# Layer 1's last 1024 tokens as one group of two halves, with seven products in place of eight

## The chip, the cores and the metric

The kernel runs on one core of a Trainium2 chip, as one program. The core has a matrix engine (TensorE, PE in the profile; its weight loads are PEld), three engines for vectors (VectorE = DVE, ScalarE = ACT, GpSimd = POOL), and SyncE (SP), which in this kernel issues every DMA transfer on one queue, in its program's order. The metric is device time in microseconds, the median of several runs.

## The reference

Sliding-window attention over 4 x 8 heads, 576 positions, head dimension 64, then two layers on the 2304 tokens (model size 512, inner size 2048):

```python
rel = pos[:, None] - pos[None, :]
mask = (rel >= 0) & (rel < 64)
attn = softmax(where(mask, scale * q @ k.T, -1e9))
x = (attn @ v).transpose(0, 2, 1, 3).reshape(2304, 512)
h = np.maximum(x @ w_in, 0.0);  x = h * h @ w_out          # layer 1
h = x @ w_in2;  out = (h * np.cos(h)) @ w_out2             # layer 2
```

All of it is float32. The kernel reaches that on TensorE with values split in two (hi, rounded to the engine's format fp32r, and lo, the difference): each product of two matrices is three passes, hi x hi, hi x lo and lo x hi. "Three passes" below means this.

## The kernel before

**Order of the work.** A class `Plan` holds every step with its engines, an estimated length, a key and its dependencies, and takes, engine by engine, the step that can begin first (near ties: by key). The result is a fixed order of instructions for each engine; at run time an engine waits at an instruction until its inputs are there, and everything behind waits with it. Buffers come from rings (`Ring`). The ring "W" has 18 slots of 8 KB per partition and holds all weights, raw words of weights and large working tiles; "g" and "r" (activations) have two buffers each, "x2" two; PSUM has four "acc" and four "q" banks. DMA completions use eight semaphores in turn.

**Units of layer 1.** The tokens go in units of 256: attention for unit n runs in two passes g (`attention`: S on L639, exponentials on L662, transposes T on L681, weighted sums O on L696), and its result X, hi and lo, feeds the first product. Layer 1 works on spans of units: (0, 2 units), (2, 1), (3, 2), (5, 2), (7, 2), that is 512, 256, 512, 512, 512 tokens. For each of 16 blocks j of 128 inner elements, `g1` makes ph (L1208: 4 blocks of model size x three passes = 12 matmuls of up to 512 columns), `UnitA.act` makes g, hi and lo (L778 to L791), and two items later `g2` adds the block to four accumulators accA (L814: 4 x 3 = 12 matmuls). At the end of a span `finish` copies accA to x2 tiles (L834, L836) and stores them to DRAM (x2_dram, in the profile x_dram, L839). Weight block j is loaded as raw 64-bit words (L336), turned to float32 (`to_f32`: two passes on ScalarE at L347 and L307, a shift and a merging custom instruction on VectorE, L359 and L363) and split (`convert_w`: hi by a cast, L307 or L311, lo at L385). A weight tile of layer 1 holds the in and out weights of one j, 16 tiles in all, kept for the whole layer.

**Layer 2** works on three pairs of 768 tokens (two halves of 384). There the first product of two blocks j goes by seven products in place of eight (Strassen's scheme in Winograd's form): the weights of the two blocks, cut in 2 x 2, are turned into seven combined pieces, four in w2a and three in w2b, and the tokens into seven pieces B11, B21, T2, T1, T3, T4, B22 (`prepare`). `convert_w2` makes w2a, w2b and the out weights w2o of two blocks during the last spans of layer 1 and stores them in DRAM (L433, L503, L509); layer 2 loads them step by step as wa, wb and wo (`load_w`, L955). `group` (L1099) runs the products x, y, z of one step in three PSUM banks: ScalarE copies x to "held" (L1115), VectorE adds it to y or z (L1122), and x goes on accumulating. Activations of the first half are used at once, those of the second half are kept in SBUF and used behind the group. `Job` (L1057) is the second product into accB.

**The lines that matter for PE** are L1208 with L814 (spans of layer 1), L1099 and L1057 (layer 2). The list of spans and the place of the attention units in it:

```python
spans = [(0, 2), (2, 1)] + [(n, 2) for n in range(3, NUA, 2)]
att_at = {0: [1], N2 - 4: [2], N2: [3, 4]}
for s in range(2, NSA - 1):
    n, k = spans[s + 1]
    att_at[N2 + (s - 1) * NJ] = list(range(n, n + k))
```

Of the kernel before, what the change touches and what calls it, by code (L numbers as in the profile page):

```python
# [28 lines left out]
def f32(ap):  # L29
    return ap.bitcast(F32)  # L30
# [56 lines left out]
class Plan:  # L87
# [12 lines left out]
    def op(self, engs, key, fn, deps=(), take=(), use=(), lat=None, gap=0, order=()):  # L100
# [96 lines left out]

START = {'ahead': 3,
# [31 lines left out]
def kernel(  # L230
# [10 lines left out]
    w2o: bass.AP,  # L241
    seq: int,
# [14 lines left out]
    TW = 2 * H  # L257
    NPAIR = NT // TW
# [22 lines left out]
        "pb": Ring(1), "sm": Ring(2), "PT": Ring(1), "br": Ring(2), "bg": Ring(2), "R": Ring(4), "h": Ring(2),  # L281
    }
# [91 lines left out]
    def convert_w(src, j, key, late, after, early):  # L374
# [15 lines left out]
        w_hi[j] = [hi, hi]  # L390
        w_lo[j] = [lo, lo]
        w_buf[j] = wb

    w2_half = {}
# [3 lines left out]
    def convert_w2(j, key, after):  # L398

        jp, q = divmod(j, 2)  # L400
        w2_half[q] = to_f32(w2, j, key, [after, w2_taken[0]], key - 3, True, False)
        if not q:
            return
        (wa, ba, oa), (wb_, bb, ob) = w2_half[0], w2_half[1]
        cvs, t = [ba, bb], {}
        bufs = {x: R["W"].buf() for x in "oab"}
# [10 lines left out]
        def oh(e, i):  # L417
            if i == 0:
                new("o", [2, 2, DM])
            copy(e, t["o"][:, i, 0], (wa, wb_)[i]()[:, 1])  # L420

        def ol(e, i):
            sub(t["o"][:, i, 1], (wa, wb_)[i]()[:, 1], f32(t["o"][:, i, 0]))

        ends = []
        prev = None
        for i in range(2):
            h = op(both(DM), key, lambda e, i=i: oh(e, i), [(oa, ob)[i], prev],
                   [] if i else [bufs["o"]], [*cvs, *([bufs["o"]] if i else [])])
# [59 lines left out]
        def blo2(e):  # L489
# [4 lines left out]
        o1 = op(d, key, s1, [oa, ob, *ends], A, cvs)  # L494
# [8 lines left out]
        st.append(dma(key, lambda e: nc.sync.dma_start(w2a[jp], f32(t["a"])), P * 8 * Q * 4,  # L503
                      [l1, l2], use=A))
# [9 lines left out]


# [33 lines left out]
    def mask_kind(t):  # L549
# [11 lines left out]
    spans = [(0, 2), (2, 1)] + [(n, 2) for n in range(3, NUA, 2)]  # L561
    x_col = [0, UA, 2 * UA] + [((n - 3) % 4) * UA for n in range(3, NUA)]
    x_before = [
        [m for m in range(n) if x_col[m] == x_col[n]][-1:] for n in range(NUA)]
# [4 lines left out]
    def attention(n, g, key, sp, k_s=None):  # L569
# [156 lines left out]

        half, off = divmod(x_col[n], 2 * UA)
        sl = slice(off, off + UA)
        cs = slice(2 * g, 2 * g + 2)
# [21 lines left out]
    class UnitA:  # L751
# [56 lines left out]
        def g2(self, j, m, t, w):  # L808
# [40 lines left out]
    class Half:  # L849
# [20 lines left out]
        def g2(self, j, m, t, w):  # L870
# [25 lines left out]
    def piece_free(p, o, c):  # L896
# [3 lines left out]
        for i in (4 * o + 2 * c, 4 * o + 2 * c + 1):  # L900
            out.append(open_b[0] if 10 <= i < 18 else g1_last[NUA - 3 if i < 10 else NUA - 1])
        return out

    def prepare(p, at, key, after):
        t0 = p * TW
        for c in range(2):
# [38 lines left out]
            split(B22, 3, l)  # L945

# [217 lines left out]

    def job_at(p, k):
        return base + p * 22.7 + 16.8 + 0.376 * (2 + k)

    units = [UnitA(n, k) for n, k in spans]
    NSA = len(spans)
# [14 lines left out]
    base = place[-1] - LAG + 1.0  # L1184
    N2 = NJ + J0
    att_at = {0: [1], N2 - 4: [2], N2: [3, 4]}
    for s in range(2, NSA - 1):
        n, k = spans[s + 1]
        att_at[N2 + (s - 1) * NJ] = list(range(n, n + k))

    w2_at, done = {}, 0
    for i in range(NA):
        if done >= 26 and len(w2_at) < NJ and done >= 26 + 6 * len(w2_at):
            w2_at[i] = len(w2_at)
        done += items[i][0].w // UA
    line = [None]

    def g1(i, key):
        u, j = items[i]
        phb, wb = R["q"].buf(), w_buf[j]  # L1200
        t = {}
        for c in range(NCC):
            def mm(e, c=c):
# [3 lines left out]
                for k, (wl, xl) in enumerate(((0, 0), (0, 1), (1, 0))):  # L1207
                    nc.tensor.matmul(  # L1208
                        t["ph"][:, 0:u.w], wb.tile[:, 0, wl, c * P:c * P + P], u.x(xl, c),
# [4 lines left out]
                         [line[0], w_hi[j][0], w_lo[j][0], *u.x_ready(c)],  # L1214
# [7 lines left out]
    def g2(i, key, g, ends=None, part=None):  # L1222
        u, j = items[i]
        t, gb, ready = g
        wb = w_buf[j]
        ends = [] if ends is None else ends
        for m in range(u.groups) if part is None else part:
            def mm(e, m=m):
# [4 lines left out]
                         [line[0], w_hi[j][1], w_lo[j][1], *ready], take, [gb, wb, *use],  # L1233
# [9 lines left out]
    for j in range(NJ):  # L1243
        key = 2.0 * (j if j < SK else 2 * j - SK) - 6.0
        key, late, early = START["conv"].get(j, (key, key, key - 3.0))
        convert_w(w1, j, key, late, w_lo[j - 4][1] if j >= 4 else None, early)
    gs = {}

    def att_key(n, g):
        if (n, g) in START["att"]:  # L1250
            return START["att"][n, g]
        if n <= 4:
            return 16.0 + 8.0 * (n - 2) + 4.0 * g, 2.0
# [186 lines left out]
```

## Time and profile before

| | us |
|---|---|
| median of three runs | 854.56 |
| the three runs | 854.49 to 854.81 |
| span of the profiled execution | 852.8 |
| PE busy in it | 845.4 |
| VectorE busy | 589.8 |
| ScalarE busy | 489.2 |
| end of layer 1's last span on PE, about | 469 |

The profile is of one execution; its span is the time between the first and the last instruction that it records, and it has no other time of its own. The granted clock is that of TensorE. The rows on which the argument rests stand in a section of their own below.

### The profile page before, as it was taken

What the parts mean: (1) busy time and instruction counts of PE and PEld (TensorE: products, weight loads), DVE (VectorE), ACT (ScalarE), POOL (GpSimd) and SP (SyncE); (2) the same over time, 40 slices, a digit from 0 to 9 for tenths busy, and PEclk for the clock granted to TensorE, in tenths of its full rate; (3) what the DMA queues carried; (4) which work ended last, traced back from release to release, by engine and by line L of the source; (5) the groups of instructions that cost most, each with busy time, mean ns of one, the idle gap of its engine ahead of it and who ended that gap; (6) DMA issues with size and microseconds to landing.
All of it is one profiled execution on the core that took longest, in us unless ns stands there. A gap on an engine that the chain in (4) does not pass through costs nothing.

```text
span 852.8 us, 14017 instructions
## 1 busy us (share of the span) xinstructions
PE 845.4 (99%) x5298; PEld 739.9 (87%) x5298; DVE 589.8 (69%) x1395; ACT 489.2 (57%) x1045; POOL 5.0 (1%) x25
## 2 busy tenths in 40 slices
PE   8999999999999999999999999999999999999998
PEld 7998889998888888888888999988999988999986
DVE  6998468765856557655713678887688886788851
ACT  6999568655565554535422655564565563555542
POOL 2000000000000000000000000000000000000000
PEclk9999999999999999999999999999999999999999
DMA  8971145637446354543931396035553043643011
GB/s 335 359 319 69 50 137 203 236 126 262 176 164 237 142 195 152 210 167 139 386 123 38 116 404 257 2 108 226 194 188 124 1 175 159 238 148 121 0 38 38
DMA packets 28596, 144.18 MB, mean 169 GB/s; under 512 B 3056, under 2 KB 3568, under 8 KB 18288
## 3 DMA queue, kind: packets, MB, share of 16 engines
q1 hardware_dynamic: 28528, 143.27, 44.9%
q8 instruction: 42, 0.69, 0.3%
q14 instruction: 26, 0.21, 0.1%
HBM read 110.76 MB, written 32.51 MB: 168 GB/s over the span
## 4 chain that ended last, share of the span: by engine, by line
PE 96%; DMA 1%; ACT 1%; DVE 1%; SPq 0%; issue 0%; ACTq 0%
PE ph L1208 23%; PE accB L1057 23%; PE accA L814 22%; PE x L1099 12%; PE z L1099 6%; PE y L1099 3%; PE O L696 2%; PE S L639 2%; PE T L681 2%; DMA raw_in_w_dram<-in_w_dram 1%; PE accA L875 1%; ACT pb L662 0%; PE T L295 0%; SPq L611 0%; ACT W_in_w_dram L307 0%
## 5 line engine op out<-in xcount | busy, mean ns | idle before, releaser
L1208 PE MATMUL ph<-X,W_in_w_dram 128*128 128x512 f32 (+1 forms) x1008 | 215.5, 361 | 0.0
L814 PE MATMUL accA<-g,W_in_w_dram 128*128 128x512 f32 (+1 forms) x912 | 204.5, 370 | 0.0
L1208 PEld LDWEIGHTS ph<-X,W_in_w_dram 128*128 128x128 f32 x1008 | 170.7, 189 | 28.5 <-issue 0.3
L814 PEld LDWEIGHTS accA<-g,W_in_w_dram 128*128 128x128 f32 x912 | 157.9, 189 | 29.1 <-issue 1.9
L778 ACT ACTIVATE r<-ph 128x512 f32<-128x512 f32 (+1 forms) x84 | 44.6, 531 | 100.4 <-PE ph L1208 97.8
L1057 PE MATMUL accB<-wo,gb_e 128*128 128x512 f32 x432 | 100.1, 389 | 0.0
L1057 PEld LDWEIGHTS accB<-wo,gb_e 128*128 128x128 f32 x432 | 81.0, 188 | 16.5
L311 DVE CAST g<-r 128x512 fp32r<-128x512 f32 (+1 forms) x55 | 21.8, 397 | 84.4 <-PE accA L814 75.1
L662 ACT ACTIVATE pb<-pb,mm 128x128 f32<-128x128 f32 x144 | 56.0, 392 | 18.8 <-DVE mm L656 18.6
L791 DVE TENSOR_TENSOR g<-r,g 128x512 fp32r<-128x512 f32 (+1 forms) x84 | 51.7, 615 | 15.7 <-ACT r L786 11.7
L1057 PE MATMUL accB<-wo,gb_a 128*128 128x512 f32 x216 | 54.5, 393 | 0.2 <-ACT x L834 0.2
L1057 PE MATMUL accB<-wo,gb_b 128*128 128x512 f32 x216 | 54.3, 393 | 0.0
L1057 PEld LDWEIGHTS accB<-wo,gb_a 128*128 128x128 f32 x216 | 40.1, 188 | 7.7 <-ACT x L834 0.6
L1057 PEld LDWEIGHTS accB<-wo,gb_b 128*128 128x128 f32 x216 | 40.2, 188 | 7.5
L1115 ACT ACTIVATE held<-x 128x384 f32<-128x384 f32 x72 | 34.4, 481 | 21.1 <-PE x L1099 21.1
L1099 PE MATMUL x<-X,wb 128*128 128x384 f32 x216 | 45.7, 337 | 0.0
L1099 PE MATMUL x<-X,wa 128*128 128x384 f32 x216 | 45.3, 335 | 0.0
L786 ACT ACTIVATE r<-r 128x512 f32<-128x512 f32 (+1 forms) x74 | 41.9, 566 | 2.3
L1099 PEld LDWEIGHTS x<-X,wa 128*128 128x128 f32 x216 | 38.7, 188 | 2.4
L1031 DVE TENSOR_TENSOR gb_e<-keep,gb_e 128x384 fp32r<-128x384 f32 x48 | 26.0, 555 | 21.2 <-ACT gb_e L307 20.9
L307 ACT ACTIVATE gb_e<-keep 128x384 fp32r<-128x384 f32 x48 | 24.2, 517 | 25.5 <-PE accB L1057 25.5
L347 ACT ACTIVATE raw_in_w_dram<-raw_in_w_dram 128x1024 f32<-128x1024 f32 x32 | 36.7, 1148 | 3.6 <-DMA raw_in_w_dram<-in_w_dram 3.5
(134 smaller groups left out, 1299.6 us busy)
## 6 DMA issues: line engine op xcount, KB each, us to landing
raw_in_w_dram<-in_w_dram SPq DMA_DIRECT2D x32, 1024.0 KB, 7.4
wa<-w2a_dram SPq DMA_DIRECT2D x24, 1024.0 KB, 7.2
wb<-w2b_dram SPq DMA_DIRECT2D x24, 768.0 KB, 5.3
qk<-in_qk_dram SPq DMA_DIRECT2D x17, 576.0 KB, 6.1
v<-in_v_dram SPq DMA_DIRECT2D x18, 512.0 KB, 4.6
w2o_dram<-w2o SPq DMA_DIRECT2D x8, 1024.0 KB, 3.9
w2a_dram<-w2a SPq DMA_DIRECT2D x8, 1024.0 KB, 4.3
wo<-w2o_dram SPq DMA_DIRECT2D x8, 1024.0 KB, 9.4
```

Of the source, the lines that this page charges most:

```text
L307: nc.scalar.activation(o, i, AF.Copy, scale=scale)
L347: nc.scalar.activation(hw, hw, AF.Prelu, scale=2.0**-112, alpha=-(2.0**32))
L662: nc.scalar.activation(t["pb"][:, e, r, i], t["pb"][:, e, r, i], AF.Exp, bias=t["mm"][:, e, r, i:i + 1], scale=-1.0, accum_out=t["sm"][:, ...
L778: nc.scalar.activation(t["r"], ph()[:, 0:w], AF.Relu)
L786: nc.scalar.activation(t["r"], t["r"], AF.Square)
L791: nc.vector.tensor_tensor(t["g"][:, 1], t["r"], f32(t["g"][:, 0]), ALU.subtract)
L814: nc.tensor.matmul(self.acc[i][:, k, :], w[:, 1, wl, m * P:m * P + P], t["g"][:, gl, :], start=(j == 0 and p == 0 and k == 0 and self.n > ...
L1031: nc.vector.tensor_tensor(t["g"][:, 1], r(), f32(t["g"][:, 0]), ALU.subtract)
L1057: nc.tensor.matmul(acc[0], t["g"][:, gl, m * P:m * P + P], wb.tile[:, k % 2, wl], start=(k == 0 and i == 0), stop=(k == NJ - 1 and i == 2))
L1099: nc.tensor.matmul(ps[x], wb.tile[:, i, wl, c * P:c * P + P], piece(o, c, xl), start=(first and c == 0 and k == 0), stop=(last and c == 1 ...
L1115: return b, op({"ACT": act_us(H)}, key - 6, lambda e: nc.scalar.activation(r_at(b), ps[x], AF.Copy), [dep, o_rooms], [b], [buf], lat=0.39)
L1208: nc.tensor.matmul(t["ph"][:, 0:u.w], wb.tile[:, 0, wl, c * P:c * P + P], u.x(xl, c), start=(c == 0 and k == 0), stop=(c == NCC - 1 and k ...
```

## The change

**What it does.** Only the first three spans stay: (0, 2), (2, 1), (3, 2). The last 1024 tokens, units 5 to 8, become one group of two halves of 512 tokens, H1 = 512. For it:

- Weights of layer 1 are packed on the host in pairs: tile 2i holds the in weights of blocks 2i and 2i + 1, tile 2i + 1 their out weights. `g1` and `g2` take theirs by `unit_in` and `unit_out`. Layer 2's weights are packed alike, so `convert_w2` makes w2a and w2b from one raw tile and w2o from the next, each by itself.
- `sums1` makes, for each pair of blocks, the four combined weight pieces, and stores these and the three plain ones in DRAM (w1s_dram). `load_in1` loads them again in each step as w1a (1 MB) and w1b (0.75 MB), as layer 2 does with wa and wb.
- Attention of units 5 and 6 (the first half) writes X as before; that of units 7 and 8 writes one unsplit tile xr. `prepare1` makes the pieces T2, T1, T3, T4, B22. All attention now lies beside the three spans, in the order of units 0, 1, 2, 3, 4, 6, 5, 7, 8.
- `group1` runs 7 products x 6 matmuls of 512 columns in each of 8 steps. Activations of the first half (g1_a.., g_b..) go straight on to the second product, `job1`, into accC_0; those of the second half are squared and stored in DRAM (kept_dram, 16 tiles of 256 KB), loaded again by `load_kept` in four pieces, split, and multiplied into accC_1 behind the group.
- The tables `MID` say at which item of the plan attention, sums and layer 2 weights enter; eight of the 16 raw tiles of layer 2 are loaded and converted beside the group.

The core of the diff:

```diff
+MID = {'att': {3: (17.0, 0), 4: (39.3, 1.7), 5: (-0.7, 0), 6: (34.8, 8), 7: (51.6, 3.0), 8: (40.3, 5.9)},
+ 'sum': (13, 16, 19, 20, 24, 35, 43, 44),
+ 'w2': (25, 32, 35, 35, 37, 37, 37, 38, 38, 38, 39, 39, 39, 41, 45, 47),
+ 'w2key': 44.5}
...
+    def unit_in(j):
+        return 2 * (j // 2)
...
+    def sums1(jp, key, after):
...
+        o = op({"DVE": dve_us(2 * DM)}, key, whole, [w_lo[u], after, s1_held[0]], C, [wb])
+        o = op(d, key, s1, [o], S, C)
+        o = op(d, key, s2, [o], use=S + C)
+        o = op(d, key, s3, [o], use=S + C)
+        o = op(d, key, s4, [o], use=S + C)
+        o = op({"ACT": act_us(2 * DM), "DVE": dve_us(2 * DM, True)}, key, hi, [o], use=S)
+        o = op({"DVE": dve_us(2 * DM)}, key, lo, [o], use=S)
+        s1_held[0] = o
+        s1_stored[jp] = [
+            dma(key, lambda e: nc.sync.dma_start(
+                w1s[jp, :, 2:6], f32(t["s"])), P * 8 * Q * 4, [o], use=S),
...
-    spans = [(0, 2), (2, 1)] + [(n, 2) for n in range(3, NUA, 2)]
-    x_col = [0, UA, 2 * UA] + [((n - 3) % 4) * UA for n in range(3, NUA)]
+    spans = [(0, 2), (2, 1), (3, 2)]
+    x_col = [0, UA, 2 * UA, 0, UA, 2 * UA, 3 * UA]
...
+    xr = R["W"].buf()
...
+    def prepare1(key, free):
...
+        for c in range(2):
+            a = dve(lambda e, c=c: tt(tmp(0, c), *whole(B11, c), ALU.add), x5[c], [tb])
+            a = dve(lambda e, c=c: tt(tmp(0, c), raw(0, c), tmp(0, c), ALU.subtract), [a, *x7[c]], [tb, xr])
+            st[T1, c] = a
+            st[T2, c] = dve(lambda e, c=c: tt(tmp(1, c), raw(1, c), tmp(0, c), ALU.subtract),
+                            [a, *x7[c + 2]], [tb, xr])
+            st[T3, c] = dve(lambda e, c=c: tt(raw(0, c), raw(1, c), raw(0, c), ALU.subtract),
+                            [a, st[T2, c]], [xr])
...
+    def load_in1(jp, key, after, later=None):
+        in1[jp] = [
+            load_w(key, f"w1a_{jp}", w1s[jp, :, 0:4], [4, 2, 2 * P], [*s1_stored[jp], *after]),
+            load_w(key, f"w1b_{jp}", w1s[jp, :, 4:7], [3, 2, 2 * P],
+                   [*s1_stored[jp], *(later or after)])]
...
+    def group1(jp, key):
...
+        def store(k, dst, b, o):
+            o = op({"DVE": dve_us(H1)}, key, lambda e: nc.vector.scalar_tensor_tensor(
+                dst(), dst(), 0.0, dst(), ALU.max, ALU.mult), [o], use=[b, hk1])
+            kept1[k] = dma(key - 3.0, lambda e: nc.sync.dma_start(kd[k], dst()), P * H1 * 4, [o],
+                           use=[b, hk1])
...
+        o = product("x", bx, pa, 0, B11, True, True)
+        r1, o_r1 = hold(bx, "x", o)
+        o = product("y", by, pa, 1, B21, True, True)
+        h11, hb, o_h = add("y", by, r1, [o, o_r1])
...
+        rest1[2 * jp] = act1(key + 0.4, h11, [hb, hk1], o_h, f"a{nm}")
+        o = product("x", bx, pa, 2, T2, False, True, [o_r1])
+        r2, o_r2 = hold(bx, "x", o)
+        oz = product("z", bz, pa, 3, T1, True, True)
...
+        o = product("x", bx, pb, 0, T3, False, True, [o_r2])
+        r3, o_r3 = hold(bx, "x", o)
+        h22, b22, o_22 = add("z", bz, r3, [oz, o_r3])
+        store(2 * jp + 1, h22, b22, o_22)
...
+        o = product("x", bx, pb, 2, T4, False, True, [o_r3])
+        rest1[2 * jp + 1] = UnitA.act(wide, lambda: ps["x"], bx, f"b{nm}", key + 1.2, o)
...
+        o = product("z", bz, pb, 1, B22, False, True, [o_22])
+        h12, b12, o_12 = add("z", bz, r2, [o, o_r2])
+        store(2 * jp, h12, b12, o_12)
...
+    def load_kept(i, key, after):
+        kload[i] = load_w(key, f"kept_{i}", kd[4 * i:4 * i + 4].rearrange("k p n -> p k n"), [4, H1],
+                          [*(kept1[k] for k in range(4 * i, 4 * i + 4)), *after])
...
-    att_at = {0: [1], N2 - 4: [2], N2: [3, 4]}
+    att_at = {0: [1], N2 - 4: [2], N2: [3, 4, 6], N2 + NJ: [5, 7, 8]}
...
+        if more and jp:
+            load_in1(jp + 1, key - 2.1, [ends[jp - 1]], [half[jp - 1], ends[jp - 1]])
+        for j in w2_at(NA + jp):
+            convert_w2(j, key + MID["w2key"], line[0])
```

**Where the last 1024 tokens begin, on PE.** Before, the unit of tokens from 1280 on (ph_52) begins like any other, an item of 12 matmuls of the first product and 12 of the second:

```order
L814 MATMUL accA_3_3_2481<-g_49_3206,W_in_w1_dram_13_1126 128x512 x3
L1208 MATMUL ph_52_3279<-X_80,W_in_w1_dram_0_436 128x512 x12
L814 MATMUL accA_3_0_2464<-g_50_3238,W_in_w1_dram_14_1135 128x512 x3
L814 MATMUL accA_3_1_2470<-g_50_3238,W_in_w1_dram_14_1135 128x512 x3
L814 MATMUL accA_3_2_2475<-g_50_3238,W_in_w1_dram_14_1135 128x512 x3
L814 MATMUL accA_3_3_2481<-g_50_3238,W_in_w1_dram_14_1135 128x512 x3
L1208 MATMUL ph_53_3312<-X_80,W_in_w1_dram_1_347 128x512 x12
L814 MATMUL accA_3_0_2464<-g_51_3277,W_in_w1_dram_15_1176 128x512 x3
```

After, the last items of the third span (accA_3) lie between the products of the group's first step (x1_0, y1_0, z1_0):

```order
L903 MATMUL accA_3_3_2646<-g_49_3548,W_in_w1_dram_13_1155 128x512 x3
L1410 MATMUL x1_0_3630<-X_80,w1a_0_3185 128x512 x6
L1410 MATMUL y1_0_3645<-X_80,w1a_0_3185 128x512 x6
L903 MATMUL accA_3_0_2577<-g_50_3598,W_in_w1_dram_15_1205 128x512 x3
L903 MATMUL accA_3_1_2592<-g_50_3598,W_in_w1_dram_15_1205 128x512 x3
L1410 MATMUL x1_0_3630<-piece_2_3542,w1a_0_3185 128x512 x6
L1410 MATMUL z1_0_3683<-x_more_3531,w1a_0_3185 128x512 x6
L903 MATMUL accA_3_2_2598<-g_50_3598,W_in_w1_dram_15_1205 128x512 x3
L903 MATMUL accA_3_3_2646<-g_50_3598,W_in_w1_dram_15_1205 128x512 x3
L1410 MATMUL x1_0_3630<-X_80,w1b_0_3210 128x512 x6
```

What moved: the first product no longer reads weights kept in SBUF (W_in_w1_dram, as the ring's tiles are named) but the loads w1a_0 and w1b_0, and tokens in the pieces X, piece_2 (T2), x_more (T1).

**A step in the middle of the group, on PE.** Before, the same kind of place is the row of items shown above. After:

```order
L1488 MATMUL accC_0_0_3779<-g1_ag2_3942,W_in_w1_dram_5_826 128x512 x3
L1488 MATMUL accC_0_1_3787<-g1_ag2_3942,W_in_w1_dram_5_826 128x512 x3
L1410 MATMUL x1_3_3953<-piece_2_3542,w1a_3_3885 128x512 x6
L1410 MATMUL z1_3_4033<-x_more_3531,w1a_3_3885 128x512 x6
L1488 MATMUL accC_0_2_3814<-g1_ag2_3942,W_in_w1_dram_5_826 128x512 x3
L1488 MATMUL accC_0_3_3822<-g1_ag2_3942,W_in_w1_dram_5_826 128x512 x3
L1410 MATMUL x1_3_3953<-X_80,w1b_3_3912 128x512 x6
L1410 MATMUL x1_4_4059<-X_80,w1a_4_3999 128x512 x6
L1410 MATMUL y1_4_4068<-X_80,w1a_4_3999 128x512 x6
L1410 MATMUL x1_3_3953<-X_80,w1b_3_3912 128x512 x6
L1488 MATMUL accC_0_0_3779<-g_bg2_4011,W_in_w1_dram_5_826 128x512 x3
L1410 MATMUL z1_3_4033<-piece_6_3551,w1b_3_3912 128x512 x6
```

What moved: in a step's 66 matmuls, 42 are of the first product (it was 48 for two blocks of 1024 tokens) and 24 of the second, for the first half alone; step 4 begins (x1_4) before step 3 has ended (x1_3, T4).

**Beside it, on SP's queue.** Before, beside the second last span, SP stores x2 tiles and layer 2's weights and loads raw words; nothing that PE will read soon, but attention's inputs:

```order
L839 DMA x2_dram<-x2_3_0_3341 128x512
L839 DMA x2_dram<-x2_3_1_3347 128x512
L433 DMA w2o_dram<-w2o_4_3268 128x2048
L839 DMA x2_dram<-x2_3_2_3388 128x512
L839 DMA x2_dram<-x2_3_3_3397 128x512
L503 DMA w2a_dram<-w2a_4_3353 128x2048
L509 DMA w2b_dram<-w2b_4_3419 128x1536
L615 DMA v_7_1_3491<-in_v_dram 128x1024
```

After, beside steps 3 and 4 of the group:

```order
L443 DMA w2o_dram<-w2o_4_4030 128x2048
L1442 DMA kept_dram<-hk1_3665 128x512
L1138 DMA w1a_5_4109<-w1s_dram 128x2048
L1442 DMA kept_dram<-hk1_3665 128x512
L1138 DMA w1b_5_4140<-w1s_dram 128x1536
L514 DMA w2a_dram<-w2a_5_4104 128x2048
L356 DMA raw_in_w2_dram_11_4173<-in_w2_dram 128x2048
L520 DMA w2b_dram<-w2b_5_4121 128x1536
L1442 DMA kept_dram<-hk1_3665 128x512
L1138 DMA w1a_6_4221<-w1s_dram 128x2048
```

What moved: each step's loads w1a and w1b now stand between the stores of layer 2's weights and of the kept activations. The load w1a_5 takes the slot of the tile w2o_4 whose store stands two rows ahead of it; w1a_6 that of w2a_5, four rows ahead.

## Rows read from the trace of the kernel before

**Rows 1.** The page: span, busy time of each engine, granted clock by slice (tenths).

```profile
span 852.8 us, 14017 instructions
...
PE 845.4 (99%) x5298; PEld 739.9 (87%) x5298; DVE 589.8 (69%) x1395; ACT 489.2 (57%) x1045; POOL 5.0 (1%) x25
...
PEclk9999999999999999999999999999999999999999
```

**Rows 2.** Waits of PE, whole span: total us, times, longest.

```profile
PE S L639 <- DMA qk<-in_qk_dram: 1.9, 2, 1.7
PE S L295 <- DVE still L290: 1.2, 1, 1.2
PE T L681 <- ACT pb L662: 0.3, 1, 0.3
PE accB L1057 <- ACT x L834: 0.2, 1, 0.2
```

**Rows 3.** The chain in order of time: start us, us, what.

```profile
65.03 2.72 PE accA L814 x12
67.75 2.72 PE ph L1208 x12
...
395.75 2.87 PE accA L814 x12
...
561.75 34.06 PE accB L1057 x150
```

**Rows 4.** Groups by line and form: instruction, count | busy us, mean ns | idle before.

```profile
L1208 PE MATMUL ph<-X,W_in_w_dram 128*128 128x512 f32 x720 | 175.4, 392 | 0.0
...
L791 DVE TENSOR_TENSOR g<-r,g 128x512 fp32r<-128x512 f32 x60 | 41.5, 692 | 14.9 <-ACT r L786 11.7 <-ACT g L307 1.8
...
L347 ACT ACTIVATE raw_in_w_dram<-raw_in_w_dram 128x1024 f32<-128x1024 f32 x32 | 36.7, 1148 | 3.6 <-DMA raw_in_w_dram<-in_w_dram 3.5
L778 ACT ACTIVATE r<-ph 128x512 f32<-128x512 f32 x60 | 35.7, 594 | 95.8 <-PE ph L1208 93.4 <-issue 1.7
...
L363 DVE CUSTOM_DVE_ANT_0 cw_in_w_dram<-raw_in_w_dram,cw_in_w_dram 128x2048 uint16<-128x2048 uint16 x16 | 19.6, 1226 | 3.7 <-ACT raw_in_w_dram L307 2.9
...
L385 DVE TENSOR_TENSOR W_in_w_dram<-raw_in_w_dram,W_in_w_dram 128x1024 fp32r<-128x1024 f32 x16 | 19.4, 1223 | 1.7 <-ACT W_in_w_dram L307 1.6
...
L311 DVE CAST g<-r 128x512 fp32r<-128x512 f32 x43 | 18.3, 426 | 79.4 <-PE accA L814 72.5 <-PE T L681 6.7
...
L791 DVE TENSOR_TENSOR g<-r,g 128x256 fp32r<-128x256 f32 x24 | 10.2, 423 | 0.8 <-ACT g L307 0.3
...
L311 DVE CAST W_in_w_dram<-raw_in_w_dram 128x1024 fp32r<-128x1024 f32 x4 | 2.8, 692 | 0.1
```

**Rows 5.** Busy time in two stretches: PE, PEld, DVE, ACT, POOL; clock, DMA share, GB/s.

```profile
45.00:65.00 20.00, 20.00 (x136) 18.53 (x135) 19.47 (x39) 19.59 (x36) 0.00 (x0) 1.00 0.76 311
...
412.00:432.00 20.00, 20.00 (x90) 16.57 (x89) 13.71 (x29) 7.32 (x13) 0.00 (x0) 1.00 0.92 361
```

**Rows 6.** The page: DMA issues, count, KB each, median us to landing.

```profile
raw_in_w_dram<-in_w_dram SPq DMA_DIRECT2D x32, 1024.0 KB, 7.4
wa<-w2a_dram SPq DMA_DIRECT2D x24, 1024.0 KB, 7.2
...
w2o_dram<-w2o SPq DMA_DIRECT2D x8, 1024.0 KB, 3.9
w2a_dram<-w2a SPq DMA_DIRECT2D x8, 1024.0 KB, 4.3
wo<-w2o_dram SPq DMA_DIRECT2D x8, 1024.0 KB, 9.4
```

**Rows 7.** DMA issues from 395 to 435 us only, columns as in rows 6.

```profile
wa<-w2a_dram SPq DMA_DIRECT2D x2, 1024.0 KB, 11.3
...
w2a_dram<-w2a SPq DMA_DIRECT2D x1, 1024.0 KB, 7.5
```

More of the change, by code (lines that the diff above doesn't have):

```diff
@@ L108, in op @@
             b.users.append(o)
+        for b in take:
+            b.taker = o
+        o.deps += [b.taker for b in use if b.taker is not None and b.taker not in o.deps]
         return o
@@ L398, in convert_w2 @@
     def convert_w2(j, key, after):
[L400 to L406, printed above, removed]
+        jp, out_part = divmod(j, 2)
+        w32, cvb, o32 = to_f32(w2, j, key, [after, w2_taken[0]], key - 3, True, False)
+        cvs, t = [cvb], {}
+        bufs = {x: R["W"].buf() for x in ("o" if out_part else "ab")}
         def new(x, shape):
@@ L725, in attention, with whole @@
         turns[turn] = o_v
+        cs = slice(2 * g, 2 * g + 2)
+        if n >= len(x_col):
+            at = (n - len(x_col)) * UA
+            new = xr.slot is None and not xr.users
+            def whole(eng):
+                if xr.tile is None:
+                    xr.tile = wp.tile([P, NCC, H1], F32, tag=f"W{xr.slot}", name="x_whole")
+                copy(eng, xr.tile[:, cs, at:at + UA], t["O"])
+            o_h = op({"ACT": act_us(2 * UA, False), "DVE": dve_us(2 * UA) + 0.11}, key + sp, whole,
+                     [o_v, s1_held[0]], [xr] if new else [], [ob] if new else [ob, xr])
+            for r in range(2):
+                x_hi[n, 2 * g + r] = x_lo[n, 2 * g + r] = o_h
+            return
         half, off = divmod(x_col[n], 2 * UA)
         sl = slice(off, off + UA)
-        cs = slice(2 * g, 2 * g + 2)
         def hi(eng):
@@ L1183, with w2_at @@
     place += [2.0 * NJ + k for k in range(NA - len(place))]
-    base = place[-1] - LAG + 1.0
+    base1 = place[-1] - LAG + 1.0
+    base = base1 + PER1
     N2 = NJ + J0
-    att_at = {0: [1], N2 - 4: [2], N2: [3, 4]}
[L1187 to L1195, printed above, removed]
+    att_at = {0: [1], N2 - 4: [2], N2: [3, 4, 6], N2 + NJ: [5, 7, 8]}
+    att_order = [0, 1, 2, 3, 4, 6, 5, 7, 8]
+    sum_at = {i: jp for jp, i in enumerate(MID["sum"])}
+    def w2_at(i):
+        return [j for j, k in enumerate(MID["w2"]) if k == i]
     line = [None]
@@ L1232, in g2 @@
             line[0] = op({"PE": u.group_us}, key + 0.5 + m / 8, mm,
-                         [line[0], w_hi[j][1], w_lo[j][1], *ready], take, [gb, wb, *use],
+                         [line[0], w_hi[uo], w_lo[uo], *ready], take, [gb, wb, *use],
                          lat=None if j == NJ - 1 else 0.0)
@@ L1289 @@
     for jp in range(2):
[L1290 to L1296 removed]
+        load_in(0, jp, base - 4.0, [gate, *w2_end])
+    load_out(0, base - 3.0, [gate, *w2_end])
+    late1 = []
+    for k in range(NJ):
+        g = rest_of(k, key_k(k) - 1.0, [job_ends1[-3]] if k > 2 else [])
+        js = job1(1, k, key_k(k), g)
+        if k >= NJ - 2:
+            late1.append(js)
+            continue
+        for f in js:
+            f()
+        job_ends1.append(line[0])
+    fills = late1
     job_ends = []
```

386 lines of the change are left out of this document (325 added, 61 removed).

## The prediction

> **What bounds the kernel now.** I read the engine shares first, then PE's waits, then the chain in order of time, then single durations, and the DMA rows last. PE (TensorE) is busy for 845.4 of the 852.8 us, and the granted clock is full speed, the 2.4 GHz level, in every slice [rows 1]. Its waits on anything sum to 3.6 us in the whole span [rows 2]. So no wait of size is there to be removed: the time falls only if PE gets less to do, and rises if something new makes PE wait. The chain in order of time gives PE's price: twelve matmuls of 512 columns take 2.72 us, and 150 in a row take 34.06 us [rows 3], 0.2268 us each. (The mean of one matmul in the groups by line is 392 ns [rows 4]; that is a length from start to modelled end, and matmuls overlap. It is no price.)
>
> The profiled span is 852.8 us and the median of the runs 854.56 us, 1.76 us more. I make the sum on the span and add 1.76 at the end.
>
> **What the change removes from PE.** Before, the last 1024 tokens are two units; the first product takes 16 blocks x 12 matmuls in each, 384. After, it takes 8 steps x 7 products x 6 matmuls, 336. The second product keeps its 384, the attention its instructions, layer 2 its own. That is 48 matmuls of 512 columns fewer: 48 x 0.2268 = **10.9 us**, the whole gain. A wait can take it back, nothing else can, since PE's other rows stay.
>
> *A rule on this price.* The Trainium skill, page "TensorE: Matmul & The Clock Gate", section "Wait — 56ns, not 53.3ns?", puts back-to-back matmuls of 512 columns 215.7 ns apart. The rows show 226.7 here; by the page the gain would be 10.4 us, by the rows 10.9. I take the rows.
>
> **What it adds, engine by engine.**
>
> *VectorE in units 0 to 2.* Eight sets of weight sums: one addition of 1024 elements (1.22 us), four of 256 (some 0.42 us by the nearest rows), a cast of 1024 (0.69 us, here or on ScalarE), a difference of 1024 (1.22 us): 4.1 to 4.8 us each, 33 to 38 us [rows 4]. Four attention units also move forward into this stretch. I added up every VectorE instruction that now stands beside these units, each by its row: 82 to 83% of PE's time there. The stretch from 45 to 65 us had VectorE at 97% and ScalarE at 98% with PE busy throughout [rows 5], so 83% need not make PE wait. The tight place is the first two sums: they stand among the last weight conversions, ahead of casts that PE needs. There VectorE's lead over PE shrinks by 2.5 us in my addition, and is still 8 us above the tightest point of the kernel before. I take 0.4 us for the whole stretch, bounds 0 (nothing can be won, PE has no wait there to lose) to 10.9 (rival C).
>
> *VectorE in the group.* A step of the group has three adds, three squares and two differences of 512, 8 x 0.69 = 5.5 us, a cast or square more, and one layer 2 weight unit, 3.8 us (out) to 6 us (in). That is at most 12.5 of the 66 x 0.2268 = 15.0 us that PE takes: hidden, and the rows of 45 to 65 us carried more. Holding a product (ScalarE, 0.6 us [rows 4]) hides behind the next product, 6 x 0.2268 = 1.4 us; layer 2 has the same steps with less cover (products of 384 columns) and its only wait is 0.2 us [rows 2].
>
> *DMA.* Sums written and read, 14.7 MB each, kept activations 4.2 MB each way: 37.8 MB more. The group with its share of layer 2 weights moves 38.3 MB in 8 x 15.0 = 119.8 us, 320 GB/s. The stretches at 45 to 65 and 412 to 432 us moved 311 and 361 GB/s with PE never idle [rows 5]. So the bytes fit, but what decides is when one load lands.
>
> *The chain of transfers in a group step.* This is the unknown. The 18 weight slots are so full in the group that each step's w1a load goes into the slot of the layer 2 tile just stored, and must wait until that store has landed; in SP's listing the load stands two or four rows behind that store. I follow the tighter kind, store w2o_4, load w1a_5, counting from PE's row accC_0_0<-g1_ag2 (t = 0; the ring of two g tiles lets VectorE go on there):
> - from t = 0 VectorE needs 0.43 + 0.69 + 1.23 + 0.69 + 1.22 = 4.3 us to the end of w2o_4 [rows 4], if its raw words are ready; the store is issued at 4.3.
> - those words come by a 1 MB load that may start when PE has read w1a_2 for the last time, 48 matmuls before t = 0, so at -10.9, and starts some 0.3 later behind the w2a store. It lands 7.4 us later by the median of such loads [rows 6], 11.3 by the slowest 1 MB loads, in the crowded stretch from 395 to 435 us [rows 7]; two ScalarE passes of 1.15 us [rows 4] and about 1 us of queueing follow: ready at 0.1 to 4.0. The third of those instructions needs them at 1.1, so the store goes at 4.3 to 7.2.
> - it lands 3.9 us [rows 6] to 7.5 us [rows 7] later: 8.2 to 14.7. SP has one more row between, the store of kept activations, whose square is ready about 8.8 (T3 ends after 30 matmuls, 6.8 us, and hold, add, square take 2.0).
> - w1a_5 is issued at 8.8 to 14.7 and lands 7.2 [rows 6] to 11.3 us [rows 7] later: 16.0 to 26.0.
> - PE needs it 96 matmuls after t = 0, at 21.8.
>
> So the spare time is 5.8 us with median transfers, and the wait 4.2 us with the slowest everywhere; the middle of both, 21.0, just makes it. The other kind (w2a store, then load) comes out at 31.0 to 36.7 by the same steps against a need at 36.8: no wait. Three of the six such loads are of the tight kind. I take 0.4 us a load, 1.2 us in all, since the group's 320 GB/s is nearer to the 311 of the stretch from 45 to 65 us than to the crowded one; bounds 0 to 3 x 4.2 = 12.6 us.
>
> *A rule on this chain.* The Trainium skill's page "DMA: Bandwidth & Descriptors", section "Anatomy of one DMA — SWDGE (gpsimd) path", speaks against the change: a transfer signals only when its last byte is confirmed, with a long delay above all where it writes to HBM. Rows 6 don't bear that out: the 1 MB stores land in 3.9 to 4.3 us, the loads in 7.2 to 9.4. The page's fit, 2 us + bytes / 436 GB/s, would give 4.4 us for either, and no wait at all: 844.1 us.
>
> *The entry.* The last PE rows of unit 2 interleave with the first products, and the four x2 stores with the load w1a_2, which itself waits for a w2a store. accC_0_2 and accC_0_3 need PSUM that the last two copies free, and these need x2 tiles whose stores SP reached before: spare 2.4 and 0.8 us. The kernel before had a raw load among its x2 stores at 393 us and PE's row grew from 2.72 to 2.87 us [rows 3]. I take 0.2 us, bounds 0 to 2.
>
> *Half 1 and the start of layer 2.* Kept activations come back in four 1 MB loads, each for four blocks, 4 x 2.72 = 10.9 us, issued a block group ahead: hidden at 11.3 too, nearly. Layer 2's first pieces and weights are asked for earlier than their use by half 1's 43.5 us. I take 0.2 us, bounds 0 to 1.5. Two boundaries of units vanish; they cost nothing before.
>
> **Sum.** 852.8 - 10.9 + 0.4 + 1.2 + 0.2 + 0.2 = 843.9; less about 0.4 for the two qk waits of the kernel before [rows 2], of which the loads now stand elsewhere in SP's row: 843.5. With 1.76: **845.3 us**, chance 0.62. Its own range is 843.2 (no new wait, and a few tenths of the old ones gone) to 848.
>
> **Rivals.**
> *A: the tight loads are late by half the bound.* 3 x 2.1 = 6.3 us instead of 1.2: 850.4 us, still faster. For it: loads of 1 MB took 11.3 us where the DMA engines were 0.9 busy [rows 5, 7]. Against it: the group is less crowded. 0.16.
> *B: slower, by the same chain.* It decides from 10.9 / 3 = 3.6 us per tight load, or 1.8 if all six wait: w1a landing at 25.4 in my count, against 16.0 to 26.0. With the slowest transfers everywhere, 12.6 us in place of 1.2: 856.7 us; with the same wait on all six, 25.2 us: 869.3. For it: SP issues in order, so a late kept store or a raw load behind it delays all that follows, and several transfers of 1 MB share the queue in each step. Against it: a slip of PE gives the next load the time that this one lacked. 0.13.
> *C: no change.* The forward-moved attention makes PE wait: twelve passes x 0.9 us = 10.9, 854.6 us. For it: a pass is a round trip PE, VectorE, ScalarE, VectorE, PE, and PE's listing holds its instructions at fixed places. Against it: in the first 65 us such passes ran beside a fuller VectorE with no wait after the first loads. 0.09.
> That the change does less than it says is excluded: PE's listing shows 48 matmuls fewer.
>
> **Chances.** 0.2% (1.7 us) is about what a measurement can tell here. Faster: the forecast's 0.62, and A's 0.16: 0.78. Same: C's 0.09 and 0.01 of B: 0.10. Slower: the rest of B, 0.12. The range takes in the forecast and A: 843.0 to 853.0; B and most of C, 2 in 10, stay out.
>
> **What would show it.** PE's matmuls of 512 columns in layer 1 fall from 1440 to 1392, PE's busy time by about 11 us. Right: PE's waits stay under 6 us, with none above 1 us on a w1a load, and the group takes 120 to 122 us. A or B: a row "PE x1 waits for DMA w1a", largest on w1a_3, w1a_5 and w1a_7, and raw loads landing in over 9 us in the group. C: waits of PE on pb, T or S between 75 and 270 us. The forecast is also wrong if the granted clock falls below 1.00 in the group, which no row of the kernel before shows, or if matmuls reading the strided w1a tile cost more than 0.2268 us.

## The result and the profile after

The changed kernel takes 845.94 us (median of 4 runs, 845.35 to 846.84) against 854.63 us (854.49 to 854.81): a ratio of 0.990, 95% interval 0.9886 to 0.9914, 8.7 us less. The forecast was 845.3 us with a range of 843.0 to 853.0. The profiled execution has a span of 844.5 us, 8.3 us under that of before.

The page of the kernel after (span, busy time, granted clock by slice), the answer to [rows 1]:

```profile
span 844.5 us, 14102 instructions
...
PE 834.1 (99%) x5250; PEld 730.7 (87%) x5250; DVE 653.4 (77%) x1481; ACT 492.0 (58%) x1051; POOL 5.0 (1%) x25
...
PEclk9999999999999999999999999999999999999999
```

PE's busy time falls by 11.3 us, the span by 8.3: PE stands idle 3 us longer. Where, PE's waits say (line and tile, what it waited for, total us, times, longest), the answer to [rows 2]:

```profile
PE S L713 <- DMA qk<-in_qk_dram: 2.4, 2, 1.8
PE accC L1488 <- ACT x L923: 2.4, 1, 2.4
PE S L309 <- DVE still L304: 1.2, 1, 1.2
PE T L755 <- ACT pb L736: 0.3, 1, 0.3
```

Three of the four are old; the qk wait at the program's start is 0.5 us longer (1.9 and 2.4; in the profiles of the runs below it is anything from none to 2.9). New is one wait of 2.4 us, of accC on a ScalarE copy. The chain in order of time (start us, us, what) around it and in the first steps of the group, for [rows 3]:

```profile
295.04 1.36 PE x L1410 x6
...
309.32 1.36 PE z L1410 x6
312.02 7.14 DMA x_dram<-x
320.87 2.76 PE x L1410 x12
...
335.87 2.72 PE x L1410 x12
...
350.83 2.72 PE x L1410 x12
```

The steps come every 14.96 us (335.87 to 350.83; 66 x 0.2268 = 14.97 was forecast). From 312.0 to 319.2 us the chain leaves PE and runs through one transfer: a store of 256 KB to x2_dram that took 7.14 us. Beside it, in the timeline (start us, us, engine, instruction; in brackets the idle time before and what ended it):

```profile
312.02 0.32 SPq L928 DMA_DIRECT2D x_dram<-x  x1
...
316.63 0.84 PE L1488 MATMUL accC<-g_ag,W_in_w_dram 128*128 128x512 f32 x3
319.24 0.60 ACT L923 ACTIVATE x<-accA 128x512 f32<-128x512 f32 x1 [3.17 <-DMA x_dram<-x]
...
319.89 0.98 PE L1488 MATMUL accC<-g_ag,W_in_w_dram 128*128 128x512 f32 x3 [2.42 <-ACT x L923]
```

The fourth copy out of accA needs the x2 tile that the second store is still reading; accC_0_3 needs the bank that this copy frees. The first store had been issued at 309.98, the load w1a_2 of 1 MB at 310.35, the second store at 312.02. The load landed at 318.5, the second store right behind it, at 319.16.

Three stretches by engine (us; PE, PEld, DVE, ACT and POOL busy, with counts; granted clock, DMA share, GB/s), for [rows 5]:

```profile
100.00:150.00 50.00, 49.96 (x506) 43.48 (x505) 39.19 (x127) 29.06 (x90) 0.00 (x0) 1.00 0.67 227
200.00:250.00 50.00, 50.00 (x452) 40.79 (x451) 43.04 (x135) 35.40 (x100) 0.00 (x0) 1.00 0.78 269
324.00:410.00 86.00, 86.00 (x381) 71.23 (x380) 62.58 (x98) 36.74 (x54) 0.00 (x0) 1.00 0.89 324
```

And the same 50 us of the kernel before:

```profile
100.00:150.00 50.00, 50.00 (x508) 43.64 (x508) 33.13 (x121) 35.38 (x105) 0.00 (x0) 1.00 0.43 148
```

PE is busy all through the attention's stretches, though VectorE went from 33.1 to 39.2 us in the first of them; and all through the group, with DMA at 324 GB/s (320 was forecast) and VectorE at 73%. Transfers landed like this in the middle of the group (count, KB, median us), for [rows 6, 7]:

```profile
raw_in_w_dram<-in_w_dram SPq DMA_DIRECT2D x6, 1024.0 KB, 7.8
w1a<-w1s_dram SPq DMA_DIRECT2D x5, 1024.0 KB, 7.7
...
w2o_dram<-w2o SPq DMA_DIRECT2D x3, 1024.0 KB, 7.4
kept_dram<-hk SPq DMA_DIRECT2D x11, 256.0 KB, 4.4
```

Layer 2 is as it was: its first product begins at 469.2 us before and 461.1 after, and 383.6 and 383.4 us remain.

### The profile page after: what moved, and what is told of

It reads as the page before. It is cut to its first block, busy times and chain, and to the rows that moved or that the text cites. A ratio compares the mean times of both kernels' runs of the same rounds, so it can differ in the third digit from the quotient of the medians.

```text
span 844.5 us, 14102 instructions
## 1 busy us (share of the span) xinstructions
PE 834.1 (99%) x5250; PEld 730.7 (87%) x5250; DVE 653.4 (77%) x1481; ACT 492.0 (58%) x1051; POOL 5.0 (1%) x25
## 4 chain that ended last, share of the span: by engine, by line
PE 96%; DMA 2%; ACT 1%; SPq 0%; DVE 0%; issue 0%; ACTq 0%
PE accB L1240 23%; PE ph L1571 13%; PE x L1282 12%; PE accA L903 12%; PE accC L1488 10%; PE z L1282 6%; PE x L1410 5%; PE y L1282 3%; PE z L1410 2%; PE O L770 2%; PE S L713 2%; PE T L755 2%; DMA raw_in_w_dram<-in_w_dram 2%; PE accA L964 1%; PE y L1410 1%; DMA x_dram<-x 1%
## 5 line engine op out<-in xcount | busy, mean ns | idle before, releaser
L1571 PE MATMUL ph<-X,W_in_w_dram 128*128 128x512 f32 (+1 forms) x624 | 124.5, 344 | 0.0
L903 PE MATMUL accA<-g,W_in_w_dram 128*128 128x512 f32 (+1 forms) x528 | 111.5, 355 | 0.0
L1571 PEld LDWEIGHTS ph<-X,W_in_w_dram 128*128 128x128 f32 x624 | 98.2, 189 | 13.4 <-issue 1.2
L903 PEld LDWEIGHTS accA<-g,W_in_w_dram 128*128 128x128 f32 x528 | 86.4, 189 | 13.3 <-issue 1.0
L1488 PE MATMUL accC<-g_k,W_in_w_dram 128*128 128x512 f32 x192 | 44.6, 391 | 0.0
L1488 PEld LDWEIGHTS accC<-g_k,W_in_w_dram 128*128 128x128 f32 x192 | 35.8, 188 | 7.8 <-DVE g_k L1388 0.5
L1282 PEld LDWEIGHTS x<-X,wb 128*128 128x128 f32 x216 | 38.5, 188 | 0.3
L1429 ACT ACTIVATE held<-x 128x512 f32<-128x512 f32 x24 | 14.3, 598 | 38.8 <-PE x L1410 38.8
```

What stands on the lines that cost most here:

```text
L903: nc.tensor.matmul(self.acc[i][:, k, :], w[:, j % 2, wl, m * P:m * P + P], t["g"][:, gl, :], start=(j == 0 and p == 0 and k == 0 and self. ...
L1282: nc.tensor.matmul(ps[x], wb.tile[:, i, wl, c * P:c * P + P], piece(o, c, xl), start=(first and c == 0 and k == 0), stop=(last and c == 1 ...
L1488: nc.tensor.matmul(acc[0][:, 0], wb.tile[:, k % 2, wl, m * P:m * P + P], t["g"][:, gl, :], start=(k == 0 and p == 0), stop=(k == NJ - 1 an ...
L1571: nc.tensor.matmul(t["ph"][:, 0:u.w], wb.tile[:, j % 2, wl, c * P:c * P + P], u.x(xl, c), start=(c == 0 and k == 0), stop=(c == NCC - 1 an ...
```

## The experiments

**The changed kernel again.**

> The changed kernel once more, beside its variants on the same chip: about 845.9 us, 8.7 us under the kernel before. If the wait at the start of the group is what differs between executions (its store's landing), the spread stays over 1 us, against 0.3 us for the kernel before.

Measured 845.43 us (843.45 to 846.88) against 854.9 for the kernel before (853.12 to 856.3), ratio 0.9891 (0.987 to 0.9912); the new wait is 2.4 us again. The kernel before spread by 3.2 us here, so the spread says nothing on that wait, and this part of the expectation has no answer. The wait was the same in both profiles of the kernel after (2.42 and 2.44 us), and its four executions here, 3.4 us apart, all show a mean granted clock of 1.000: what sets them apart stays open.

**The gain itself: the 48 matmuls given back.**

```diff
-                    for k, (wl, xl) in enumerate(((0, 0), (0, 1), (1, 0))):
+                    reps = 3 if o == B11 and c == 0 else 1
+                    for k, (wl, xl) in list(enumerate(((0, 0), (0, 1), (1, 0)))) * reps:
```

> The 48 matmuls given back: in each of the group's eight steps the first three matmuls of the B11 product run three times, each time from a cleared bank, so 6 matmuls of 512 columns more a step and the same numbers out. Theory (the change's gain is 48 matmuls at 0.2268 us and nothing else): 10.9 us more than the changed kernel, 856.8 us, 2.2 us above the kernel before. Rival (the group's steps wait for transfers anyway, so that PE's work there is partly free): less than 8 us more, under 854 us.

Measured 856.75 us (855.94 to 857.76, ten runs), ratio 1.0022 (1.0012 to 1.0031). That is 11.3 us over the kernel after beside it and 10.8 over its first median. The plainest evidence is the step of the group, in the chain of this run (the first product of one step and of the next):

```profile
340.27 4.08 PE x L1411 x18
356.59 4.08 PE x L1411 x18
```

A step takes 16.32 us in place of 14.96, which is 1.36 us for 6 matmuls, 0.2267 each, and 10.9 for the eight steps. So the price holds, and nothing of PE's time in the group is free. (Layer 2's first product also begins 10.9 us later, at 472.0 in place of 461.1. That this is the same number is chance: PE's waits are 1.8 us less in this profile, and a stretch at a lower clock, shown in the last section, costs about as much.) It also shows what the change is without those matmuls: 1.9 us slower than the kernel before.

**The new wait, by another buffer.** The third span's copies go to one 8 KB slot with four places:

```diff
+            xs = R["W"].buf() if self.n == 3 else None
             for i, b_acc in enumerate(self.acc_b):
-                b = R["x2"].buf()
+                b = xs or R["x2"].buf()
...
+                    if xs:
+                        t["x"] = part1(xs, "x2_3", i).unsqueeze(1)
...
```

> The third span's four result copies get one 8 KB slot with four places in place of two x2 buffers in turn, so no copy waits for a store. Theory (PE's 2.4 us at the group's start is the fourth copy waiting for the second store, which took 7.1 us to land): the wait of accC on ACT x goes, the span falls by 2.4 us to about 842.1, the time to 843.5, and the runs lie closer together. Rival (the wait is only the first in a row: w1a_2, which landed 1.25 us before PE would have wanted it, is late next): a wait on w1a_2 of 1 to 2 us appears and the time stays above 845.

Measured 844.2 us (843.67 to 844.5), ratio 0.988 (0.9862 to 0.9897). PE's waits in that kernel:

```profile
PE S L713 <- DMA qk<-in_qk_dram: 2.9, 2, 1.5
PE S L309 <- DVE still L304: 1.2, 1, 1.2
PE T L755 <- ACT pb L736: 0.3, 1, 0.3
```

The wait is gone and no wait on w1a_2 takes its place; layer 2 begins at 458.6, 2.5 us earlier. The median is 1.2 us under that of the kernel after beside it, whose spread of 843.45 to 846.88 holds it, and 1.7 under its first median; what settles the point is the wait, not the median. The four runs lie 0.8 us apart. All four x2 stores stand behind the load w1a_2 now and take 6.7 to 6.9 us; nobody waits for them.

**The new wait, by SP's order alone.** (In part: `load_in1` also hands the new argument on to `load_w`, and w1b then follows its w1a.)

```diff
-            load_in1(jp + 1, key - 2.1, [ends[jp - 1]], [half[jp - 1], ends[jp - 1]])
+            load_in1(jp + 1, key - 2.1, [ends[jp - 1]], [half[jp - 1], ends[jp - 1]],
+                     [x2_done[3, 1]] if jp == 1 else [])     # order only: SP issues it later
```

> Only SP's order at the group's start: the load w1a_2 (1 MB) goes behind the second x2 store and one store of kept activations, and w1b_2 behind the fourth x2 store. Theory (the 256 KB store was slow because the 1 MB load stood just ahead of it): the second store lands in 3 to 5 us in place of 7.1, the wait on ACT x falls to 0 to 0.5 us; w1a_2 is issued some 3 us later and may cost PE 0 to 2 us. Time 843.5 to 845.5. Rival (the store is slow because of all the traffic there, whatever its place): it still takes about 7 us, the wait stays at 2 us or more, time 845.9 or above.

Measured 843.51 us (842.61 to 844.15), ratio 0.987 (0.9854 to 0.9886): the lowest median here, though its runs overlap with those of the kernel above. Transfers issued from 309 to 313.2 us, in the kernel after and in this one (the two x2 stores and w1a_2; KB, median us):

```profile
w1a<-w1s_dram SPq DMA_DIRECT2D x1, 1024.0 KB, 8.2
x_dram<-x SPq DMA_DIRECT2D x2, 256.0 KB, 5.0
```

```profile
w1a<-w1s_dram SPq DMA_DIRECT2D x1, 1024.0 KB, 7.1
x_dram<-x SPq DMA_DIRECT2D x2, 256.0 KB, 2.9
```

PE's wait on ACT x is 0, that on w1a_2 is 0.5 us:

```profile
PE x L1410 <- DMA w1a<-w1s_dram: 0.5, 1, 0.5
```

In the kernel after the first of these two stores had no load right ahead of it and landed in 2.8 us (5.0 is the median of 2.8 and 7.1); the second, behind the load, took 7.1. Ahead of the load they take 3.4 and 2.4 us. The third and fourth stores of this run now stand behind the load, and they take 6.4 and 4.7. In all eight profiles of the changed kernel and its variants, the first x2 store issued behind w1a_2 lands 0.64 to 0.71 us after that load has landed, however long the load takes (6.5 to 8.2 us). So it is the place behind the 1 MB load that makes the store slow, not the traffic as such.

**How much time the loads w1a had to spare.** (In part, as above.)

```diff
-            load_in1(jp + 1, key - 2.1, [ends[jp - 1]], [half[jp - 1], ends[jp - 1]])
+            load_in1(jp + 1, key - 2.1, [ends[jp - 1]], [half[jp - 1], ends[jp - 1]],
+                     [kept1[2 * jp - 2]] if jp > 1 else [])
```

> Only SP's order in the middle of the group: the loads w1a_3 to w1a_7 go behind the second store of kept activations of their step, 3 to 6 us later than before, and w1b right behind them. In the changed kernel these loads landed 2.7 to 4.7 us ahead of their first product. Theory (that is all the spare time there is, and a load that comes later makes PE wait): waits of PE x on DMA w1a of 0 to 3 us in each of five steps, 3 to 10 us in all, time 849 to 856, and each step is that much longer. Rival (there is more spare time than the landings show, since PE's later start moves the whole chain): under 1 us in all, time 845 to 846.5.

Measured 850.17 us (849.08 to 853.89), ratio 0.9946 (0.9931 to 0.9961), 4.2 us over the first median of the kernel after, which did not run beside it (the kernel before did, at 854.35): in the theory's range, near its lower end. The profiled execution is the slowest of the four (853.89), so its sizes are not those of the median. In it PE is shown waiting for two of the five loads, w1a_4 and w1a_6 (timeline, PE's first product on each):

```profile
356.88 1.66 PE L1410 MATMUL x<-X,w1a 128*128 128x512 f32 x6 [0.62 <-DMA w1a<-w1s_dram]
...
388.06 1.65 PE L1410 MATMUL x<-X,w1a 128*128 128x512 f32 x6 [0.85 <-DMA w1a<-w1s_dram]
```

That is 1.5 us, less than I expected from the landings, since the loads landed in 5.2 to 7.1 us here. It is not all: a short wait hides behind the modelled end of the matmul before it (w1a_7 landed 0.04 us ahead of its first product, and no idle time is shown). The steps tell more. From the first product on w1a_2 to that on w1a_7 this execution takes 77.5 us (325.98 to 403.44), the kernel after 74.8 (322.10 to 396.91): some 2.6 us for late loads, and about 1 us more is lost behind the group. Some of the rest is the clock, which is 0.91 in the first 20 us and again in a stretch that begins with the old wait (2.65 us in this execution):

```profile
300.00:320.00 20.00, 19.72 (x87) 15.99 (x86) 16.39 (x27) 9.22 (x15) 0.00 (x0) 1.00 0.81 282
320.00:340.00 20.00, 17.63 (x71) 14.40 (x72) 11.21 (x20) 8.12 (x13) 0.00 (x0) 0.91 0.72 271
```

The other three executions (849.08 to 850.87) show mean granted clocks of 0.999 to 1.000, which leaves the clock less than 1 us of them; the one at 1.000 took 849.47, 3.5 us over the kernel after. So most of the 4.2 us of the median is waiting.

**VectorE beside the attention: 33 us more.**

```diff
+        def whole3(e):
+            whole(e)
+            for _ in range(2):
+                nc.vector.tensor_tensor(
+                    t["w"], f32(wb.tile[:, :, 0]), f32(wb.tile[:, :, 1]), ALU.add)
...
-        o = op(d, key, s2, [o], use=S + C)
+        o = op(d, key, again(s2), [o], use=S + C)
...
```

> The weight sums cost VectorE twice as much and more: in each of the eight sets the addition of 1024 elements is made three times and the four of 256 twice, the same numbers out; 8 x (2 x 1.22 + 4 x 0.42) = 33 us more on VectorE beside the attention and the first three spans. Theory (VectorE had room there: 172.6 us busy in the 215 us from 75 to 290): no new wait of PE above 1 us in all, time 845 to 846.9. Rival (80% was already close to what the attention's round trips bear): PE waits on T, S or g of 3 us and more between 60 and 290 us, time above 849.

Measured 869.24 us (866.08 to 873.1), ratio 1.0175 (1.0151 to 1.0199): 23 us more, and my theory falls. PE's waits (the first five):

```profile
PE T L771 <- DVE pb L762: 10.8, 7, 2.3
PE ph L1587 <- DVE X L840: 3.4, 1, 3.4
PE accC L1504 <- ACT x L939: 2.4, 1, 2.4
PE O L786 <- DVE PT L325: 2.4, 2, 1.8
PE S L729 <- DMA qk<-in_qk_dram: 2.0, 2, 1.2
```

and two stretches:

```profile
100.00:150.00 50.00, 42.38 (x392) 35.33 (x391) 46.24 (x123) 27.07 (x82) 0.00 (x0) 1.00 0.52 171
150.00:175.00 25.00, 21.57 (x204) 20.99 (x204) 20.62 (x55) 13.16 (x36) 0.00 (x0) 0.86 0.49 186
```

VectorE is at 92% from 100 to 150 us, and PE idle for 7.6 of these 50 us. The waits are the attention's round trip: T waits for pb, which VectorE normalizes late, O for PT, the first product for X. On top the granted clock is 0.86 from 150 to 175 us, among PE's waits (3.4 us the longest, up to 158.7), so part of that stretch ran at 1.2 GHz. In this profile the span is 22.7 us longer than that of the kernel after: PE's idle time grows by 17.9, and the clock takes about 3.5 (0.14 of 25 us). The five executions have mean clocks of 0.988 to 0.996, so the clock's part is 3.5 to 10 us among them.

**VectorE beside the attention: 13 us more.** Without the two extra additions of 1024 (`whole` in place of `whole3`).

> As the run with 33 us more of sums, but only the four additions of 256 elements are made twice in each set: 8 x 4 x 0.42 = 13.4 us more on VectorE. Theory (VectorE has a margin in the attention's stretch, and the 33 us went beyond it: they cost 23 us, after a first part that was free): 0 to 4 us, time 846 to 850. Rival (there is no margin; each microsecond more on VectorE beside the attention costs 0.7 us): 9.4 us, time about 855.

Measured 851.44 us (850.35 to 852.26), ratio 0.9955 (0.9938 to 0.9971): 5.5 to 6.0 us more, between the two theories.

```profile
100.00:150.00 50.00, 49.04 (x495) 42.30 (x494) 44.84 (x132) 28.46 (x86) 0.00 (x0) 1.00 0.66 225
200.00:250.00 50.00, 48.50 (x440) 38.72 (x439) 44.53 (x140) 33.69 (x92) 0.00 (x0) 1.00 0.71 246
```

With 13.4 us more the first stretches of 89 and 90% appear, and PE loses 1.0 and 1.5 us in them. Of the loss 2.7 us are PE's waits on pb, X and PT in this profile; its busy time is 4.0 us longer besides. About 1.8 of these 4.0 are the clock, not in these stretches but behind the wait of 2.1 us at the group's start:

```profile
320.00:340.00 20.00, 17.88 (x72) 14.32 (x72) 10.47 (x19) 8.53 (x14) 0.00 (x0) 0.91 0.88 328
```

All four executions have a mean clock of 0.998, which is 1.7 us of 850. The same stretch at 0.91 occurs in the run with the 48 matmuls given back, where VectorE's work is unchanged, so I don't count it as VectorE's price. Without it the 13.4 us cost about 4 us, the upper end of the theory; the 2.2 us of busy time that are left I can't explain. The curve is bent: no wait at 78 and 86%, 5.5 to 6.0 us (about 4 without the clock) for the first 13.4, some 17.5 with the clock for the next 20. There was little margin left in the kernel after, but no fixed share marks its end: in a shorter stretch with attention in it VectorE was at 94% there, and PE did not wait:

```profile
240.00:260.00 20.00, 20.00 (x201) 16.31 (x200) 18.77 (x57) 12.07 (x34) 0.00 (x0) 1.00 0.86 290
```

## Why the prediction was right, and where its steps were not

- **48 matmuls, 10.9 us: right.** Layer 2 begins 8.1 us earlier, which is 10.9 less the 2.4 of the new wait and 0.5 of the qk wait; giving the matmuls back made the group's eight steps 10.9 us longer. By the 215.7 ns of the Trainium skill's page "TensorE: Matmul & The Clock Gate" (section "Wait — 56ns, not 53.3ns?") the estimate would have been 10.4. The steps of 14.96 us here are 226.7 ns a matmul, and the measurement decides.
- **The chain of a store and a load, 1.2 us: it cost nothing.** Counted as in the prediction (t = 0 at 345.39, 24 matmuls ahead of the 350.83 of the chain, where T3 of step 3 begins), w2o_4 was stored at t = 4.3 as worked out, took 7.4 us to land, w1a_5 was issued at 11.7 and landed 5.5 us later, at 17.2, against 21.8. The spare time was about 4.5 us, by my bounds -4.2 to 5.8. What was off is the upper bound: I added the slowest store and the slowest load, but this load is issued when the store has landed, and so finds the queue emptier. w1a_5 and w1a_7, which waited for such a store, landed in 5.5 and 5.2 us; w1a_4 and w1a_6, issued behind a raw load and two stores that were still under way, took 8.3 and 9.7.
- **Which loads are tight: wrong.** I had called w1a_3, w1a_5 and w1a_7 tight, but w1a_3 was issued 4.0 us before the w2o store ahead of it landed, so it did not wait for that, and the least spare time was that of w1a_6. The five loads w1a_3 to w1a_7 landed 2.6 to 4.5 us ahead of their first product; w1a_2, without the new wait, would have landed about 1.2 ahead. Rival B's price was not reached. In the run with later loads it is w1a_4 and w1a_6 that PE is shown waiting for, the kind that the prediction expected to make no wait; delays of 3 to 6 us brought that about. The other figure of the prediction, 844.1 us by a time of 4.4 us for 1 MB, does not fit these rows: 1 MB took 5.2 to 9.7 us as w1a and 4.8 to 8.5 as stores of w2a and w2o.
- **The entry, 0.2 us with bounds 0 to 2: 2.4 us, above the bound.** This is the term that was mis-sized. I had named the place (the x2 stores with w1a_2 among them) and the spare time of 0.8 us for accC_0_3, but took the price from the kernel before, where a raw load among such stores had cost 0.15 us [rows 3], and gave the store's landing no term of its own. There the raw load landed in 5.5 us and was issued 2.4 us ahead of the store behind it, which landed 0.7 us after it, in 3.8. Here w1a_2 took 8.2 us, because the queue was fuller or for another reason that no run separates, and stood 1.7 us ahead of the store; 0.65 us after the load makes 7.1. The comparison missed that the store takes what is left of the load's time. A 256 KB store behind the 1 MB load took 7.1 us, ahead of it 2.4. The Trainium skill's page "DMA: Bandwidth & Descriptors", section "Queues, rings and completion order", says that each DMA engine takes its descriptors in the order of the ring; the two runs agree (7.1 and 2.4 us).
- **VectorE beside the attention, 0.4 us with bounds 0 to 10.9: 0 us, but for a wrong reason.** PE had no wait there. I argued from the stretch of 45 to 65 us, where VectorE was at 97% and PE did not wait [rows 5]. That work was mostly weight conversion (by summed lengths 15.3 us, where the attention's steps had 3.6), so it says little on a stretch with more of the attention. The waits in the two runs with more sums (T on pb, O on PT, the first product on X) fit the reading that what counts is how late the attention's own short steps come when they stand among others; no run changed their order, so this is argued, not shown. In stretches of 50 us PE lost 1.0 to 1.5 us at 89 to 90%, and 15% of its time at 92%. Rival C, given 0.09, was nearer than that: 13 us more work on VectorE cost 5.5 us of the 8.7 that the change had won, about 4 without the clock.
- **VectorE in the group, bytes, half 1, layer 2's start: right.** 73% of the stretch, 324 GB/s, no wait, 383.4 us as before.
- **The qk waits, -0.4 us: +0.5.** They belong to the first 20 us and differ from one execution to the next.
- **The signs.** PE's waits came to 6.3 us where the prediction wanted under 6 for being right, by the entry and the qk waits. Two of the raw loads beside the group took over 9 us (9.9 and 10.1), a sign named for A and B, and no wait on w1a came of it.

Together: 10.9 - 2.4 - 0.5 = 8.0 us of the span's 8.3. The forecast of 1.2 for the chain and 0.4 for VectorE happened to pay for the entry: that the total came within 0.6 us is partly luck.

## What to carry to other kernels

A small store on which a buffer depends should not stand behind a large load on the same queue: move the load back by one place, or give the copies buffers of their own; either took the wait of 2.4 us away here (moving the load brought 0.5 back on the load itself). The worst case of a chain is not the sum of its steps' worst cases when one step starts only after the other has left the queue. And an engine's share in a stretch says little on whether it makes others wait: ask whose work it is. Beside the attention PE lost time at 89 to 92% over 50 us, though not in 20 us at 94%; beside weight conversions it lost none at 97%.

## What the runs showed that was not expected

- A wait of PE does not always cost the clock, and its length does not tell which. The wait at the group's start was 2.38, 2.42 and 2.44 us in three profiles (33 us more on VectorE, the kernel after twice), and the granted clock stayed at 1.00 (2.4 GHz) behind it. It was 1.97, 2.12 and 2.65 us in three others (matmuls given back, 13 us more on VectorE, later loads), and the 20 us around its end have 0.91. The stretch in the run with the matmuls given back:

```profile
320.00:340.00 20.00, 18.62 (x75) 15.25 (x76) 11.18 (x19) 8.16 (x13) 0.00 (x0) 0.91 0.77 287
```

- On SP's one queue the profiles show every transfer landing after the one issued ahead of it: of the 251 transfers of the kernel after, none passed another.
- The kernel before spread by 0.3 us in the four runs beside the result and by 3.2, 2.3 and 2.6 us in the 13, 9 and 7 runs beside the variants; differences of about a microsecond between variants, as between the two that mend the entry (844.2 and 843.5), stay open.
